# Loading late weights straight into freed weight buffers, and timing evictions, stores and divisions by modelled transfer landings, in a fused attention and MLP kernel

## The chip, the cores and the metric

The kernel runs on one core of one Trainium2 chip. The metric is the device time of one execution in microseconds (us). Kernels are compared by the median of their runs.

A core has five engines, each with an instruction queue that it works through strictly in order: TensorE (PE in the profile; its weight loads are PEld), VectorE (DVE), ScalarE (ACT), GpSimd (POOL) and SyncE (SP). In this kernel SP issues every DMA. An instruction that waits for a semaphore holds up all that stands behind it in the same queue.

## The reference

A gated mix of a sliding-window attention block and an MLP over the same 2048 tokens of width 512:

```python
def _A_ref(x, wqkv, wo):
    H = 32; Dh = D // H; W = 256
    qkv = (x @ wqkv).reshape(B, S, 3, H, Dh) ...
    scores = jnp.einsum("bhqd,bhkd->bhqk", q, k) * (Dh ** -0.5)
    mask = (idx[:, None] - idx[None, :] >= 0) & (idx[:, None] - idx[None, :] < W)
    p = _softmax(jnp.where(mask, scores, -1e9), axis=-1)
    o = jnp.einsum("bhqk,bhkd->bhqd", p, v)
    return o.transpose(...).reshape(B, S, D) @ wo

def _B_ref(x, w1, b1, w2, b2):
    h = _gelu(x @ w1 + b1)
    return h @ w2 + b2

g = _sigmoid((x * gate_w).sum(-1, keepdims=True))
return g * a + (1 - g) * b
```

Shapes: S = 2048, D = 512, F = 1792, all in float32.

## The kernel before

**Precision.** Every dense product is computed as three matmuls (`mm3`, lines 122 to 129): each operand is split into a high part, rounded to the PE's fp32r format, and a low part, the remainder, and the products high*high, high*low and low*high are added. So each weight is held as two tiles. ACT writes the high part (line 275) and DVE or POOL the low part by a subtraction (line 278), from a raw tile that a DMA has brought.

**Stages.** First q, k and v for four blocks of 512 tokens (`qkv`). Then two streams share the PE. The attention stream runs over 8 groups of 4 heads, each over the 16 blocks of 128 keys: `sm` tiles (scores for the row maximum, `att_max`, line 652; DVE reduces each into `M`, line 656), `st` tiles (transposed scores, `att_exp`, line 708; ACT takes the exponential into `pt`, line 737), and every fourth block a batch of `pv` products (`att_pvs`, line 764), which are copied out as `nd` (lines 784 and 787). The dense stream is the MLP in eight turns, `TURNS`: the first half of F for token blocks 3, 0, 1, 2 and the second half for 2, 0, 1, 3. A turn computes seven `u` tiles with w1, takes each through a gelu of seven steps on ACT and DVE (`gelu`; it ends with `h`, lines 921 and 924), and then four `y` tiles with w2. Each `y` is evicted by DVE (`y_end`, line 1012) as `yo` = 0.5 y + `ya`, and `yo` is stored to DRAM (YA for the first half, YB for the second); `ya` is the bias in the first half and the stored YA row block in the second. Last come the output projection and the mix (`final`).

**Divisions.** Every second head group `att_norm` divides 16 numerators: it loads the denominators (`den`), takes the reciprocal (line 807), stores it (RD), loads it back in a broadcast form (`rb`) beside the numerators (`num`), multiplies (line 819) and stores the result (OT).

**What sets the order.** Nothing is reordered by a compiler. A planner in the kernel's Python code keeps a clock, `now[0]`, and emits the instructions of all engines in the order in which its model would run them. `put(e, ns, fn, wait, due, req, key)` queues an operation for DVE, ACT or POOL: it may be emitted from `now + wait` on, once all keys of `req` are marked; among those that may start the earliest due time goes first. `after(ns, fn)` calls a function later. `scores()` yields the attention stream, `dense()` the MLP stream; the loop at the end chooses between them by `owed`, the dense work that is due, within the bounds SLACK (1400 ns that dense may run ahead) and OVER (2000 ns that it may be behind).

**What the planner takes for a landing.** `send` emits a DMA on SP and adds 500 ns (ISSUE) to a line of issue. What depends on a transfer is called a fixed time later: `landed(ns, ...)`. For a division that is 6000 ns (`den`), 4500 ns (RD) and 9500 ns (`num`, `rb`), each after the last issue (DIVS). A `yo` is stored 4600 ns and the next-but-one `ya` loaded 4000 ns (HOLD) after its eviction is emitted. An eviction does not ask whether the store that used its buffer, or the load of its `ya`, has landed; nor do the `sm` and `st` matmuls ask for the landing of `qd` and `ks`. The hardware semaphores do: an instruction that comes too early waits at the head of its queue.

**Eight lanes.** The DMAs of SP take eight semaphores in turn. Each issue waits until the DMA eight places before it has landed, and until its own data are there, and then the DMAs behind it may go.

**Buffers.** Split weights lie in one pool, `w`, of 14 buffers, each with both parts (two times 128x512 float32). The late weights (w1, w2 and `wo`, the list `later`) are loaded as the weights of the stage before are used for the last time, at least 4000 ns (PACE) apart: up to 152 us on the plan's clock (RAWS) to halves of attention's `pt` buffers, after that to two `raw` buffers, which `slots` counts; a third load waits until the low part of one is computed and a pause REST has gone by. The gelu has two `x1` and two `sq` buffers, and `yo` shares `sq`.

## Time and profile before

| | us |
|---|---|
| median of 3 runs | 715.34 |
| lowest, highest | 712.29, 717.89 |
| profiled execution | 719.64 |
| its span, first to last instruction | 717.7 |

The profile is that of one execution; times in it are microseconds from the span's start. PE is busy in nearly all of the span, so what can be won is the time in which PE sits idle or runs at a lower clock. The profile writes idle time in square brackets behind the instruction that ended it, with what released it. PEclk is the granted clock, 1.00 being full speed. The stretch from 0 to about 100 us is the q, k and v work, 100 to 650 us holds both streams, and the output projection is the end.

### The profile page before, as it was taken

The numbers are of one execution on the slowest core, as the hardware profiler recorded it, in microseconds if no ns is written. First come the engines' busy times: TensorE is split into PE (matmuls) and PEld (weight loads), VectorE is DVE, ScalarE is ACT, GpSimd is POOL, SyncE is SP. The second block draws the span as 40 slices with busy tenths as digits, with TensorE's granted clock in tenths as the row PEclk, the third lists the DMA queues.
The fourth block names the chain that finished last, engine by engine and source line by source line (L and its number), as shares of the span: only waits on it lengthen the run. The fifth ranks groups of instructions, "written<-read, shape, count | busy, mean of one in ns | idle before, by whom it ended". The sixth has DMA issues, their size and how long they took to land.

```text
span 717.7 us, 17515 instructions
## 1 busy us (share of the span) xinstructions
PE 698.1 (97%) x6129; PEld 603.4 (84%) x6129; DVE 516.7 (72%) x1560; ACT 419.9 (59%) x972; POOL 362.6 (51%) x853
## 2 busy tenths in 40 slices
PE   9999999999899999999999999989999999999998
PEld 7888888878788888888888887878888887888786
DVE  4732425798668977986898799749967985884662
ACT  4434532378447945864696588338745863794740
POOL 4200001568665765795587668636865785540000
PEclk9999999998999999999999999999999999999999
DMA  8979899895896899899986998995899789766562
GB/s 289 360 240 384 279 360 294 260 287 168 233 262 149 213 254 269 227 237 290 249 192 169 235 248 198 254 269 125 207 251 256 191 219 266 204 199 192 183 210 103
DMA packets 178103, 169.99 MB, mean 237 GB/s; under 512 B 56544, under 2 KB 122848, under 8 KB 178016
## 3 DMA queue, kind: packets, MB, share of 16 engines
q1 hardware_dynamic: 178016, 168.87, 84.4%
q8 instruction: 49, 0.80, 0.5%
q14 instruction: 38, 0.31, 0.2%
HBM read 111.68 MB, written 61.34 MB: 241 GB/s over the span
## 4 chain that ended last, share of the span: by engine, by line
PE 82%; DMA 7%; DVE 6%; issue 2%; ACT 2%; SPq 1%; POOL 0%; DVEq 0%; POOLq 0%; ACTq 0%
PE sm L652 8%; PE st L708 8%; PE pv_sm L764 6%; PE u L127 6%; PE y L129 6%; PE y L127 6%; PE y L128 6%; PE u L128 5%; PE u L129 5%; PE qk L127 4%; PE qk L129 4%; PE qk L128 4%; DVE sm L656 3%; PE pv_st L764 2%; PE a L127 2%
## 5 line engine op out<-in xcount | busy, mean ns | idle before, releaser
L656 DVE CUSTOM_DVE_ANT_1 sm<-sm,mask 128x320 f32<-128x320 f32 (+4 forms) x512 | 232.5, 484 | 57.5 <-PE sm L652 52.5
L724 POOL TENSOR_SCALAR_AFFINE_SELECT pt<-pt 64x256 f32<-64x256 f32 (+1 forms) x538 | 205.1, 401 | 131.0 <-ACT pt L737 119.9
L737 ACT ACTIVATE pt<-st 128x320 f32<-128x320 f32 (+4 forms) x512 | 200.7, 426 | 116.2 <-PE st L708 114.9
L652 PE MATMUL sm<-kd,qd 96*128 96x320 f32 (+4 forms) x512 | 147.7, 301 | 5.1 <-DVE M L656 3.3
L708 PE MATMUL st<-qs,ks 128*128 128x320 f32 (+4 forms) x512 | 146.8, 299 | 3.2 <-issue 2.0
L688 POOL CAST qs<-tt 4x256 fp32r<-4x256 f32 x256 | 127.6, 498 | 27.9 <-DVE tt L680 16.2
L652 PEld LDWEIGHTS sm<-kd,qd 96*128 96x128 f32 x512 | 97.0, 189 | 22.0 <-DVE M L656 6.8
L708 PEld LDWEIGHTS st<-qs,ks 128*128 128x128 f32 x512 | 97.8, 191 | 14.5 <-issue 2.7
L129 PE MATMUL y<-w,h 128*128 128x512 f32 x224 | 85.0, 379 | 1.8 <-DVE h L924 1.8
L127 PE MATMUL y<-w,h 128*128 128x512 f32 x224 | 84.8, 379 | 0.0
L128 PE MATMUL y<-w,h 128*128 128x512 f32 x224 | 84.8, 378 | 0.0
L764 PE MATMUL pv_sm<-pt,vbuf 64*32 64x320 f32 (+4 forms) x1408 | 76.4, 357 | 3.2 <-DVE M L656 3.1
L127 PE MATMUL u<-mx,w 128*128 128x512 f32 x196 | 77.4, 395 | 0.1
L764 PE MATMUL pv_st<-pt,vbuf 64*32 64x320 f32 (+4 forms) x1408 | 75.7, 357 | 0.0
L129 PE MATMUL u<-mx,w 128*128 128x512 f32 x196 | 74.3, 379 | 0.0
L128 PE MATMUL u<-mx,w 128*128 128x512 f32 x196 | 74.2, 379 | 0.0
L764 PEld LDWEIGHTS pv_sm<-pt,vbuf 64*32 64x32 f32 x1408 | 52.2, 109 | 23.7 <-DVE M L656 5.3
L656 DVE DVE_READ_ACCUMULATOR2_ANT M<- 128x1 f32 x512 | 71.5, 140 | 0.0
L434 DVE TENSOR_TENSOR qke<-qk,qke 128x512 fp32r<-128x512 f32 x32 | 22.1, 691 | 41.0 <-ACT qke L431 34.7
L431 ACT ACTIVATE qke<-qk 128x512 fp32r<-128x512 f32 x32 | 19.1, 597 | 52.0 <-PE qk L129 32.4
L129 PEld LDWEIGHTS y<-w,h 128*128 128x128 f32 x224 | 42.2, 188 | 8.2 <-DVE h L924 2.2
L764 PEld LDWEIGHTS pv_st<-pt,vbuf 64*32 64x32 f32 x1408 | 46.9, 109 | 0.0
(150 smaller groups left out, 1294.2 us busy)
## 6 DMA issues: line engine op xcount, KB each, us to landing
kd<-SK SPq DMA_DIRECT2D x32, 384.0 KB
qs<-SQ SPq DMA_DIRECT2D x64, 192.0 KB
mx<-XT SPq DMA_DIRECT2D x24, 512.0 KB
SQ<-qke SPq DMA_DIRECT2D x16, 512.0 KB
SK<-qke SPq DMA_DIRECT2D x16, 512.0 KB
ND<-nd SPq DMA_DIRECT2D x32, 256.0 KB
raw_w<-in_B_w_dram SPq DMA_DIRECT2D x28, 256.0 KB
qd<-SQ SPq DMA_DIRECT2D x32, 192.0 KB
```

Of the source, the lines that this page charges most:

```text
L127: nc.tensor.matmul(p, lh, rh, start=first, stop=False)
L128: nc.tensor.matmul(p, lh, rl, start=False, stop=False)
L129: nc.tensor.matmul(p, ll, rh, start=False, stop=last)
L431: nc.scalar.activation(halves(e[:, h]), p, AF.Copy)
L434: nc.vector.tensor_sub(halves(e[:, 1 - h]), p, halves(f32(e[:, h])))
L652: nc.tensor.matmul(v, qd[0:96, n, pr, 128 * j:128 * (j + 1)], two(kd[0:96, n, pr, k1 - w:k1]), start=True, stop=True)
L656: nc.vector.tensor_tensor_reduce(v, v, two(mask[:, 320 - w:320]), 1.0, -3e38, ALU.add, ALU.max, M[:, 2 * (b % RB) + hb, pr:pr + 1])
L688: nc.gpsimd.tensor_copy(dst, src.unsqueeze(1).broadcast_to([4, 2, RB, 32]))
L708: nc.tensor.matmul(pairs(p[:, :w]), ks[:, slot(g_, kb // NB), pr, at:at + 128], two(qs[:, pr, k0:k0 + w]), start=True, stop=True)
L724: nc.gpsimd.affine_select(out=v, in_=v, pattern=[[0, v.shape[1]], [1 - 2 * e, 64]], compare_op=ALU.is_ge, fill=0.0, base=-e, channel_multi ...
L737: nc.scalar.activation(halves(pt[:, hf, pr, :w]), sorted_(p[:, :w]), AF.Exp, scale=SCALE)
L764: nc.tensor.matmul(pv[r // 64][32 * i:32 * i + 32, q - c * T:e - c * T], vts[g_, b // NB][r:r + 64, v:v + 32], rhs(r), start=start, stop=s ...
```

## The change

The same matmuls, transfers and vector operations are issued; two low parts move from DVE to POOL (12 subtractions of w on POOL before, 14 now). What changes is where the weights lie, and when the planner emits what.

- **Weights.** The pool `w` is replaced by 14 places for high parts (`wh`) and 15 for low parts (`wl0` to `wl14`), held by name in `idle_low`. When a weight has been used for the last time, `drop` returns its low place. A late weight is loaded straight to such a place; its low part goes to a second one, and then the first is returned. A load needs two idle places, and loads may follow each other every 1200 ns (PACEL). After 140 us (RAWS) the engine for a low part is the one of DVE and POOL that is less behind; before, it is POOL. The two `raw` buffers go, and `x1` gets a third.
- **Landings.** The planner models eight lanes. A transfer starts when its lane is free and ends after a time by kind: 5000 ns (LOADS), 7000 ns for broadcast and scattered ones (SLOW), 4000, 4400 and 3100 ns for `nd`, `den` and RD; 1200 ns (MARGIN) are added before anything relies on it.
- **Waits in the plan.** An eviction is emitted once its `ya` has landed and the store that used its buffer has; `sm` and `st` are emitted once `qd` and `ks` have; the divisions go by the landings above. A `yo` is stored 200 ns after its eviction and the next `ya` loaded 600 ns after.
- **Bounds.** SLACK and OVER become 4000 ns.

```diff
-    line = [0.0]
+    line, lanes, sent = [0.0], [0.0] * 8, [0]
 
-    def send(to, by):
+    def send(to, by, ns=LOADS):
 
         nc.sync.dma_start(to, by)
-        line[0] = max(line[0], now[0]) + ISSUE
-
-    def landed(ns, fn, *args):
-
-        after(line[0] + ns - now[0], fn, *args)
+        k = sent[0] = (sent[0] + 1) % 8
+        at = max(line[0], now[0], lanes[k])
+        line[0], lanes[k] = at + ISSUE, at + ns
+
+    def landed(fn, *args):
+
+        after(lanes[sent[0]] + MARGIN - now[0], fn, *args)
+
+    def arrive(key):
+
+        mark(key, lanes[sent[0]] + MARGIN)
...
+    def low_tile(dtype, name):
+
+        s = idle_low.pop(0)
+        return sb.tile([128, T], dtype, tag=f"wl{s}", bufs=1, name=name), s
+
+    def high_tile(dtype, name):
+
+        return sb.tile([128, T], dtype, tag="wh", bufs=14, name=name)
+
+    def drop(key):
+
+        idle_low.append(wt[key][2])
...
         else:
-            spare.clear()
-            raw = sb.tile([128, T], F32, tag="raw", bufs=2, name=f"raw_{kind}{i}")
+            raw, slots[key] = low_tile(F32, f"raw_{kind}{i}")
...
-        paced[0] = max(now[0], paced[0] + PACE)
+        paced[0] = max(now[0], paced[0] + (PACE if now[0] < RAWS else PACEL))
...
     def load_now():
-        if now[0] >= RAWS:
-            if slots[0] - slots[1] == 2:
-                return after(500, load_now)
-            slots[0] += 1
+        if len(idle_low) < 2:
+            return after(300, load_now)
         key = asked.pop(0)
         load_raw(key)
-        if now[0] >= RAWS:
-            landed(LAND, split, key, nc.vector, True)
-        else:
-            after(LAND0 + 3000, split, key, nc.gpsimd)
+        landed(split, key, nc.gpsimd if now[0] < RAWS else None)
...
     def load_qd(g_, c):
         ready(c, g_, 0)
         put_pairs([f32(qd[48 * s:48 * s + 48, slot(g_, c)]) for s in range(2)], SQ[c], g_)
+        arrive(("qd", g_, c))
...
+            reqs = [("ya", n * NB + b)]
...
-                y = sb.tile([128, D], F32, tag="sq", bufs=2, name=f"yo{t}_{half}{b}")
+                y, k = sq_of(f"yo{t}_{half}{b}", ("yos", n, b))
+                reqs += k
...
-            after(HOLD, ya_load, n * NB + b + 2)
...
+            def then():
+                after(YALD, ya_load, n * NB + b + 2)
+                if n + 1 < len(TURNS):
+                    after(YST, store)
+                else:
+                    ybs[t * NB + b] = y
+                    mark(("y", half, t, b))
+            put("V", 604, ev, 130, 500, req=reqs, key=("ye", n, b), then=then)
...
-                        yield (rings["st"][0], *rows_of(u // NKB, u % NKB, i))
+                        yield (rings["st"][0], ("ks", u // NKB, u % NKB // NB), *rows_of(u // NKB, u % NKB, i))
...
-                        yield (rings["sm"][0],)
+                        yield (rings["sm"][0], ("qd", gm, bm // NB))
...
-RAWS = 152000.0
+RAWS = 140000.0
+LOWS = 15
...
-DIVS = ((6000, 4500, 9500), (5000, 2500, 7000))
-REST = 1000.0
...
-SLACK = 1400.0
-OVER = 2000.0
+SLACK = 4000.0
+OVER = 4000.0
```

In a division the calls read `landed(first)`, `landed(both)` and `landed(times)` now, with the kinds 4400 for `den`, 3100 for RD and SLOW for `num` and `rb` given to `send`.

**DVE at the last gelu of the turn that loads the second w2.** The rows are in DVE's own order, with the program's names: `h2_12` and `h2_13` are low parts of the gelu's results, `x1h` a step before, `w2_13` the low part of a late weight, `num3_1` a division's product, `sm` a reduction of scores and `M` its result. Before:

```order
L924 TENSOR_TENSOR h2_12_6316<-x1h2_12_6316_6320,h2_12_6316 128x512
L918 SCALAR_TENSOR_TENSOR x1h2_13_6383_6389<-sqh2_13_6383_6390,x1h2_13_6383_6389 128x512
L278 TENSOR_TENSOR w2_13_6454<-raw_w213_6322,w2_13_6454 128x512
L924 TENSOR_TENSOR h2_13_6383<-x1h2_13_6383_6389,h2_13_6383 128x512
L819 TENSOR_TENSOR num3_1_6416<-num3_1_6416,rb3_1_6418 128x512
L656 ISA sm5_4_3_6541,M5_4_6482<-sm5_4_3_6541,mask_72 128x320
```

The low part of the turn's last weight stands between the last two gelu results, four to ten rows ahead of the first eviction. The same place now:

```order
L684 ISA sm5_3_1_6500,M5_0_6275<-sm5_3_1_6500,mask_72 128x320
L684 ISA M5_0_6275 128x1
L684 ISA sm5_3_0_6506,M5_0_6275<-sm5_3_0_6506,mask_72 128x320
L684 ISA M5_0_6275 128x1
L961 TENSOR_TENSOR h2_13_6410<-x1h2_13_6410_6417,h2_13_6410 128x512
L684 ISA sm5_3_3_6527,M5_0_6275<-sm5_3_3_6527,mask_72 128x320
```

No late weight stands there any more: DVE's last one in this turn, `w2l12`, stands 78 rows ahead of `h2_13` (916 against 994 from the queue's start), and `w2l13` went to POOL. `h2_12` stands 32 rows ahead of the first eviction `yo2_10`, where it stood 10 ahead.

**SP at the first stores of YB.** `yo2_10` and `yo2_11` are the first two evicted tiles of that turn. Before:

```order
L140 DMA ks_74<-SK3_1_94 48x8x128
L140 DMA ks_74<-SK3_1_94 48x7x128
L140 DMA ks_74<-SK3_1_94 48x2x64
L140 DMA vbuf_158<-SV2_97 128x8x34
L140 DMA ND1_2_113<-nd4_1_6598 128x512
L140 DMA mx40_6384<-XT0_99 128x1024
L140 DMA ya2_12_6681<-YA2_141 128x512
L140 DMA YB2_145<-yo2_10_6627 128x512
```

And now:

```order
L140 DMA mx40_6411<-XT0_99 128x1024
L140 DMA YB2_145<-yo2_10_6562 128x512
L140 DMA ya2_12_6599<-YA2_141 128x512
L140 DMA ks_74<-SK3_1_94 48x8x128
L140 DMA ks_74<-SK3_1_94 48x7x128
L140 DMA ks_74<-SK3_1_94 48x2x64
L140 DMA vbuf_158<-SV2_97 128x8x34
L140 DMA ND1_2_113<-nd4_1_6654 128x512
```

The store of `yo2_10` and the load of `ya2_12` stand ahead of the `ks`, `vbuf` and `ND` transfers, behind which they stood. On DVE the eviction that takes `yo2_10`'s buffer, `yo2_12`, stands 37 rows behind `yo2_10`, where it stood 29 rows behind.

**PE ahead of the first `st` that needs the third block of `ks`.** `st0_8_0` is that matmul; `y3_00` and `y3_01` are dense tiles. Before:

```order
L127 MATMUL y3_01_2155<-w2_3_1845,h3_3_1789 128x512
L128 MATMUL y3_01_2155<-w2_3_1845,h3_3_1789 128x512
L129 MATMUL y3_01_2155<-w2_3_1845,h3_3_1789 128x512
L652 MATMUL sm1_4_1_2216<-kd_76,qd_75 128x320
L708 MATMUL st0_8_0_2219<-qs_73,ks_74 128x320
```

And now:

```order
L127 MATMUL y3_01_2206<-w2h3_1853,h3_3_1777 128x512
L128 MATMUL y3_01_2206<-w2l3_2000,h3_3_1777 128x512
L129 MATMUL y3_01_2206<-w2h3_1853,h3_3_1777 128x512
L680 MATMUL sm1_4_1_2250<-kd_76,qd_75 128x320
L127 MATMUL y3_01_2206<-w2h4_1864,h3_4_1856 128x512
L128 MATMUL y3_01_2206<-w2l4_1933,h3_4_1856 128x512
L129 MATMUL y3_01_2206<-w2h4_1864,h3_4_1856 128x512
L736 MATMUL st0_8_0_2259<-qs_73,ks_74 128x320
```

One dense product, three matmuls, has come ahead of `st0_8_0`. Between the last `sm` of head group 0 (`sm0_15_2`, which reads the `kd` buffer that SP writes next) and `st0_8_0` stand 36 `y` matmuls where there were 33; the other work between the two is the same.

## Prediction

> **What bounds the kernel now.** I read the totals first, then the waits of PE and of DVE, then the timeline around each PE wait.

> ```profile
> span 717.7 us, 17515 instructions
> PE 698.1 (97%) x6129; PEld 603.4 (84%) x6129; DVE 516.7 (72%) x1560; ACT 419.9 (59%) x972; POOL 362.6 (51%) x853
> ```

> PE is the bound: only 717.7 - 698.1 = 19.6 us of the span are free of matmuls. No work is taken away, so the change can win only PE's idle time and what follows from it. Who ends that idle time (us in total, times, longest):

> ```profile
> PE sm L652 <- DVE M L656: 3.3, 4, 1.3
> PE pv_sm L764 <- DVE M L656: 3.1, 2, 2.7
> PE st L708 <- issue: 2.0, 1, 2.0
> PE y L129 <- DVE h L924: 1.8, 1, 1.8
> ```

> PE waits for DVE most times: a score tile's PSUM buffer comes free when DVE has reduced it. DVE's own waits for transfers are therefore the next view:

> ```profile
> DVE yo L1012 <- DMA YB<-yo: 5.2, 2, 3.3
> DVE num L819 <- issue: 3.0, 2, 2.0
> DVE yo L1012 <- PE sm L652: 2.7, 1, 2.7
> DVE yo L1012 <- DMA YA<-yo: 2.1, 1, 2.1
> DVE yo L1012 <- DMA ya<-YA: 1.7, 1, 1.7
> DVE num L819 <- DMA rb<-RD: 1.2, 1, 1.2
> ```

> Evictions (`yo`) stand 5.2 + 2.7 + 2.1 + 1.7 = 11.7 us at the head of DVE's queue, the divisions' multiplications (`num`) 4.2. The largest case in the timelines of SP, DVE and PE (start, length, engine, what; idle before in brackets):

> ```profile
> 464.75 0.42 SPq L140 DMA_DIRECT2D YB<-yo  x1
> 469.50 0.69 DVE L1012 SCALAR_TENSOR_TENSOR yo<-y,ya 128x512 f32<-128x512 f32 x1 [3.25 <-DMA YB<-yo]
> 470.71 0.30 PE L764 MATMUL pv_sm<-pt,vbuf 64*32 64x64 f32 x2 [2.74 <-DVE M L656]
> ```

> The store of the first `yo` is issued at 464.75 and lands some 4.7 us later; the third eviction needs its buffer and waits 3.25 us; the reductions behind it come late, and PE stands 2.74 us. Then the clock falls (columns: stretch, its length, busy time of PE, PEld, DVE, ACT, POOL, granted clock, DMA):

> ```profile
> 160.70:167.50 6.80, 5.93 (x15) 4.84 (x16) 4.01 (x7) 4.17 (x9) 5.65 (x8) 0.50 0.67 146
> 191.40:194.80 3.40, 3.40 (x67) 1.77 (x73) 0.56 (x2) 0.44 (x1) 0.95 (x3) 0.50 1.06 280
> 471.30:474.70 3.40, 3.40 (x75) 2.50 (x58) 0.26 (x2) 0.00 (x0) 0.00 (x0) 0.50 1.11 298
> ```

> The granted clock is 0.50 in three stretches, 13.6 us together, each behind a PE wait. Half of that, up to 6.8 us, is lost on top of the idle time.

> **The change part by part.** The sum is made against this execution, 719.64 us (its span and 1.9 around it). It lies 4.3 above the median, 715.34.

> *Evictions and stores.* The PE waits behind a `yo` that waits:

> ```profile
> 206.86 0.40 PE L652 MATMUL sm<-kd,qd 96*128 96x320 f32 x1 [0.50 <-DVE M L656]
> 329.97 1.55 SPq L140 DMA_DIRECT2D YA<-yo  x1
> 334.58 0.69 DVE L1012 SCALAR_TENSOR_TENSOR yo<-y,ya 128x512 f32<-128x512 f32 x1 [2.66 <-PE sm L652]
> 335.79 0.40 PE L652 MATMUL sm<-kd,qd 96*128 96x320 f32 x1 [1.08 <-DVE M L656]
> 337.66 0.30 PE L764 MATMUL pv_sm<-pt,vbuf 64*32 64x64 f32 x2 [0.40 <-DVE M L656]
> 664.87 0.73 PE L708 MATMUL st<-qs,ks 128*128 128x320 f32 x2 [0.98 <-ACT nd L784]
> ```

> The eviction at 334.58 is put down to an `sm`, but it starts 4.6 us after a YA store was issued, as the one above came 4.75 after its store; I count it here. The change issues the store 200 ns after an eviction instead of 4600 after its emission, ahead of the `ks` loads (SP's order), and emits the next user of the buffer 37 instead of 29 DVE rows later. PE's part: 0.50 + 1.08 + 0.40 + 2.74 + 0.98 = 5.70, with half of the last slow stretch, 1.70, 7.4 us. Bounds: 3.7, if half returns behind other landings, and 7.4. I take 7.4, because both distances grow in the order. What is late next is the reduction itself.

> *Landing of `ks`.* The SP and PE rows:

> ```profile
> 160.57 11.46 SPq L140 DMA_DIRECT2D kd<-SK  x2
> 183.01 0.32 SPq L140 DMA_DIRECT2D mx<-XT  x1
> 183.38 1.72 SPq L140 DMA_DIRECT2D ks<-SK  x3
> 190.22 0.38 PE L708 MATMUL st<-qs,ks 128*128 128x320 f32 x1 [2.00 <-issue]
> 168.38 0.38 PE L127 MATMUL u<-xt,w 128*128 128x512 f32 x1
> 168.59 0.38 PE L128 MATMUL u<-xt,w 128*128 128x512 f32 x1
> ```

> SP holds `kd` until PE has read the old tile, then `mx` until the XT stores have landed, and `ks` stands behind both. The plan models neither stop. By PE's order only three matmuls of 0.21 us (start to start, 168.38 to 168.59) come in between: 0.65 of the 2.00 goes. Bounds: 0, and 2.00 + 1.70 with its slow stretch. I take 0.65, what the order shows.

> *Late weights.* At the last gelus of the turn that loads the second w2:

> ```profile
> 443.73 0.81 DVE w L278
> 446.52 0.40 PE L652 MATMUL sm<-kd,qd 96*128 96x320 f32 x1 [0.47 <-DVE M L656]
> 449.26 0.48 PE L129 MATMUL y<-w,h 128*128 128x512 f32 x1 [1.76 <-DVE h L924]
> ```

> The first row is of the chain of work that ended last: a weight's low part, 0.81 us, in DVE's queue ahead of the `h` for which PE stands. In the new order no weight is split there, and `h2_12` stands 32 rows ahead of the first eviction, not 10. PE's waits are 2.23 us; I take 2.0, bounds 0 and 2.23. The split costs the same, on ACT and, two more times, on POOL. The loads now come in a burst: five raw loads among nine consecutive issues. Behind them stand `qs`, a division's loads and `kd`. No row shows that; the nearest is the `ks` stop, 2.0 us, or 3.7 with its slow stretch; below, nothing. I charge 2.0.

> *The first gelus beside attention.*

> ```profile
> 159.22 0.40 PE L652 MATMUL sm<-kd,qd 96*128 96x320 f32 x1 [0.60 <-DMA qd<-SQ]
> 161.57 0.80 PE L127 MATMUL u<-xt,w 128*128 128x512 f32 x1 [1.20 <-DVE sqh L912]
> ```

> With half of 6.80 that is 5.2 us. The plan now asks for `qd`, and lets dense run further ahead, but DVE's work there is the same. Bounds 0 and 5.2; I take the middle, 2.6, since one of the two causes is met. The wider SLACK and OVER I cost at nothing else: they move matmuls between two streams, and either covers the other.

> *Divisions.* They are now called sooner: 8.2 us after `rb` is issued instead of 10.0, 5.6 instead of 6.5 after `den`, where lanes are free. PE's share in them before, and one more wait of an eviction:

> ```profile
> 556.50 0.40 PE L652 MATMUL sm<-kd,qd 96*128 96x320 f32 x1 [0.93 <-DVE nd L787]
> 603.93 0.40 PE L652 MATMUL sm<-kd,qd 96*128 96x320 f32 x1 [1.30 <-DVE M L656]
> 314.22 0.60 SPq L140 DMA_DIRECT2D rb<-RD  x1
> 322.30 0.77 DVE L819 TENSOR_TENSOR num<-num,rb 128x512 f32<-128x512 f32 x1 [1.22 <-DMA rb<-RD]
> ```

> This `rb` took 8.1 us, about what the plan now allows. I charge 1.0, bounds +0.93 won and 17.5 lost (the slower rival). Of the 1.30 I take half, 0.6, bounds 0 and 1.3, for DVE there waited for PE's own `y`.

> Sum: 7.4 + 0.65 + 2.0 - 2.0 + 2.6 - 1.0 + 0.6 = 10.25, which gives 709.4 for an execution like this one. The median before lies 4.3 lower, by waits of the same kind that partly did not happen; I take half of it off: 707.2.

> [...] The slow stretches of 3.40 us follow PE waits of 2.00 and 2.74. [...]

> **Rivals.**

> *DVE takes the place of the transfers.* For it speaks this window:

> ```profile
> 350.00:400.00 50.00, 50.00 (x503) 43.95 (x502) 46.64 (x149) 38.40 (x88) 39.54 (x90) 1.00 0.83 198
> ```

> DVE is busy 93% of it, and what it does not lose to landings it has to do anyway. Against it: PE lost nothing in that stretch. If half of the evictions, weights and gelus (12.0) returns, 6.0, the time is 713.2.

> *The clock does not follow the waits.* If slow stretches come at another cause's bidding, 1.7 of the evictions and 1.7 of the gelus stay: 710.6. Against it: three of three stand behind a wait.

> *The change doesn't do what it says, and DVE waits for divisions instead.* With 1.8 us less at 12 multiplications and 0.9 less at 16 reciprocals, DVE would stand up to 36 us more; PE lost 5.70 for 11.7 at the evictions, so 0.49 of that, 17.5, less the 1.0 charged: 723.7, slower. It decides from the point at which most `rb` land later than 8.2 us after their planned issue. For it: the 8.1 above. Against it: at 13 of 16 multiplications DVE did not wait at all, and a plan with lanes waits longer when they are full.

> **How the numbers follow.** My forecast has 0.48, the DVE rival 0.30, the clock 0.08, the divisions 0.14. The measurement can tell about 1% from no change: faster is below 708.2, slower above 722.5. So 0.48 faster, 0.38 the same, 0.14 slower. The range: all gains at their best, no charges: 7.4 + 3.7 + 2.23 + 5.2 + 1.3 + 0.93 = 20.8, 698.9, rounded to 700; evictions at 3.7, the others 0, the burst at 3.7 and divisions at 1.0: 720.6, on the median 718.5. I take 700 to 718; the slower rival is left out.

> **What would show it.** Right: no DVE wait of an eviction for YA or YB; no wait of a `y` matmul for `h`; fewer stretches at 0.50. `st` for the third `ks` still waits a microsecond or more. Wrong: new waits of `num` or `den` for `rb` or `den`, PE waits behind the raw loads, or PE idle time near 19.6 us again.

## The result, and the profile after

The changed kernel takes 703.39 us (median of 6 runs, 701.76 to 705.12), the kernel before 715.31 in the same runs: ratio 0.9839, 95% interval 0.9805 to 0.9872. It is faster by 1.6%, inside the predicted range and 3.8 us under the predicted 707.2. The profiled execution took 704.36 us, 15.28 less than that of before; that execution of before was a slow one, 4.3 us above its median, so 3.4 of the 15.28 go beyond the 11.9 between the medians. The totals of its page:

```profile
span 702.4 us, 17477 instructions
PE 691.5 (98%) x6129; PEld 594.1 (85%) x6129; DVE 514.4 (73%) x1558; ACT 416.5 (59%) x972; POOL 364.9 (52%) x855
```

The span without matmuls is 702.4 - 691.5 = 10.9 us, where it was 19.6: 8.7 less. PE's busy time is 6.6 less for the same 6129 matmuls: no stretch at half clock is left before the end, where there were 13.6 us. Together 15.3. Who ends the waits now, in the views of PE's and of DVE's waits (us in total, times, longest):

```profile
PE st L736 <- DMA ks<-SK: 1.7, 1, 1.7
...
PE st L736 <- ACT nd L812: 0.8, 1, 0.8
PE sm L680 <- DVE M L684: 0.8, 2, 0.5
...
PE y L129 <- DVE h L961: 0.5, 1, 0.5
```

```profile
DVE yo L1056 <- DMA ya<-YA: 3.7, 2, 2.1
...
DVE yo L1056 <- DMA YA<-yo: 1.8, 1, 1.8
```

The waits of `pv_sm` for `M` are gone, those of `sm` fell from 3.3 to 0.8 us, that of `y` for `h` from 1.8 to 0.5. Evictions still stand 5.5 us for transfers (11.7 before, with the 2.7 that was put down to an `sm`), but PE pays nothing for it that the rows show. No PE wait stands right behind the first two of the three cases. One stands behind the third; DVE's, ACT's and PE's rows there:

```profile
647.45 0.69 DVE L1056 SCALAR_TENSOR_TENSOR yo<-y,ya 128x512 f32<-128x512 f32 x1 [2.06 <-DMA ya<-YA]
...
647.99 1.91 ACT L922 ACTIVATE ot<-ot 128x512 fp32r<-128x512 f32 x3 [3.06 <-DMA ot<-OT]
649.81 0.58 ACT L812 ACTIVATE nd<-pv_st 128x512 f32<-128x512 f32 x1
...
650.44 0.40 PE L736 MATMUL st<-qs,ks 128*128 128x320 f32 x1 [0.80 <-ACT nd L812]
```

PE waits for `nd`, which stands in ACT's queue behind three `ot`, and ACT waited 3.06 us for their load. So this wait comes from the loads of the output projection and not from the eviction.

The largest wait that is left is the one for the third block of `ks`. SP and PE:

```profile
179.94 0.32 SPq L140 DMA_DIRECT2D mx<-XT  x1
180.31 2.46 SPq L140 DMA_DIRECT2D ks<-SK  x3
...
186.69 0.37 PE L736 MATMUL st<-qs,ks 128*128 128x320 f32 x1 [1.73 <-DMA ks<-SK]
```

`ks` goes as soon as `mx` has gone, as before, and its first transfer is issued 6.4 us ahead of PE's start. This wait is not there in every profile of such a kernel: see e9.

### The profile page after: what moved, and what is told of

It is laid out like the page before. It is cut to its first block, busy times and chain, and to the rows that moved or that the text cites. A ratio compares the mean times of both kernels' runs of the same rounds, so it can differ in the third digit from the quotient of the medians.

```text
span 702.4 us, 17477 instructions
## 1 busy us (share of the span) xinstructions
PE 691.5 (98%) x6129; PEld 594.1 (85%) x6129; DVE 514.4 (73%) x1558; ACT 416.5 (59%) x972; POOL 364.9 (52%) x855
## 4 chain that ended last, share of the span: by engine, by line
PE 85%; DMA 7%; DVE 2%; ACT 2%; issue 1%; POOL 1%; SPq 1%; POOLq 0%; DVEq 0%; ACTq 0%
PE sm L680 9%; PE st L736 8%; PE pv_sm L792 7%; PE y L127 6%; PE y L129 6%; PE y L128 6%; PE u L127 6%; PE u L128 5%; PE u L129 5%; PE qk L127 4%; PE qk L129 4%; PE qk L128 4%; PE a L127 2%; PE a L129 2%; PE a L128 2%; PE v L127 2%
## 5 line engine op out<-in xcount | busy, mean ns | idle before, releaser
L752 POOL TENSOR_SCALAR_AFFINE_SELECT pt<-pt 64x256 f32<-64x256 f32 (+1 forms) x538 | 208.9, 408 | 110.6 <-ACT pt L765 99.7
L765 ACT ACTIVATE pt<-st 128x320 f32<-128x320 f32 (+4 forms) x512 | 191.9, 427 | 108.3 <-PE st L736 105.0
L736 PE MATMUL st<-qs,ks 128*128 128x320 f32 (+4 forms) x512 | 143.1, 297 | 2.9 <-DMA ks<-SK 1.7
L716 POOL CAST qs<-tt 4x256 fp32r<-4x256 f32 x256 | 123.9, 484 | 27.5 <-DVE tt L708 15.9
L129 PE MATMUL y<-w2h,h 128*128 128x512 f32 x224 | 85.1, 380 | 0.8 <-DVE h L961 0.5
L127 PE MATMUL y<-w2h,h 128*128 128x512 f32 x224 | 85.1, 380 | 0.0
L128 PE MATMUL y<-w2l,h 128*128 128x512 f32 x224 | 84.8, 378 | 0.0
L127 PE MATMUL u<-mx,w1h 128*128 128x512 f32 x196 | 76.9, 393 | 0.2 <-DVE sqh L949 0.2
L129 PE MATMUL u<-mx,w1l 128*128 128x512 f32 x196 | 74.3, 379 | 0.0
L128 PE MATMUL u<-mx,w1h 128*128 128x512 f32 x196 | 74.2, 379 | 0.0
L792 PE MATMUL pv_sm<-pt,vbuf 64*32 64x320 f32 (+4 forms) x1408 | 73.3, 346 | 0.1
L453 ACT ACTIVATE qke<-qk 128x512 fp32r<-128x512 f32 x32 | 19.1, 598 | 51.5 <-PE qk L129 28.6
L129 PEld LDWEIGHTS y<-w2h,h 128*128 128x128 f32 x224 | 42.2, 188 | 7.3 <-DVE h L961 1.3
```

The lines of the kernel that those rows point to most:

```text
L127: nc.tensor.matmul(p, lh, rh, start=first, stop=False)
L128: nc.tensor.matmul(p, lh, rl, start=False, stop=False)
L129: nc.tensor.matmul(p, ll, rh, start=False, stop=last)
L453: nc.scalar.activation(halves(e[:, h]), p, AF.Copy)
L716: nc.gpsimd.tensor_copy(dst, src.unsqueeze(1).broadcast_to([4, 2, RB, 32]))
L736: nc.tensor.matmul(pairs(p[:, :w]), ks[:, slot(g_, kb // NB), pr, at:at + 128], two(qs[:, pr, k0:k0 + w]), start=True, stop=True)
```

## The experiments

Each kernel was timed beside the kernel before on the same chip, in three groups: c1 and e1 to e3; e4 to e7; e8 to e11. Three of them (c1, e4, e9) came out level with the changed kernel, so they mark it on their chips: 703.91, 702.61 and 702.86 us; costs below are against these. The changed kernel itself was not timed again beside them; by its ratio to the kernel before, 0.984, the costs of e1 to e3 would come out 1.5 us higher, that of e8 0.8 higher and those of e5 to e7 0.5 lower. "Plan" is the planner's own clock (`now[0]`) at the end of its loop, in us: what the kernel's code takes the PE stream to need, no measured time. "Clock" is what half clock took from a run on average, at most, since PE may also idle in such a stretch: (1 - mean granted clock) x span, from the clocks listed with every run.

| kernel | median us | runs | before | ratio (95%) | plan | clock |
|---|---|---|---|---|---|---|
| before, beside c1 to e3 | 713.95 | 29 | | | 686.7 | 4.1 |
| changed | 703.39 | 6 | 715.31 | 0.984 (0.981 to 0.987) | 686.7 | 0.4 |
| c1 margin 50 ns more | 703.91 | 6 | 713.95 | 0.986 (0.982 to 0.990) | 686.6 | 0.5 |
| e1 evictions undone | 708.68 | 12 | 713.95 | 0.995 (0.992 to 0.998) | 685.9 | 1.1 |
| e2 late stores, asking | 709.64 | 12 | 713.95 | 0.994 (0.992 to 0.997) | 689.5 | 1.2 |
| e3 narrow bounds | 711.31 | 12 | 713.95 | 0.996 (0.993 to 0.999) | 692.9 | 1.1 |
| e4 early stores, not asking | 702.61 | 6 | 714.57 | 0.982 (0.979 to 0.985) | 686.7 | 0.0 |
| e5 qd, ks not asked for | 706.65 | 6 | 714.57 | 0.989 (0.985 to 0.992) | 688.4 | 3.9 |
| e6 slow weights | 712.68 | 12 | 714.57 | 0.996 (0.994 to 0.998) | 694.8 | 4.2 |
| e7 late divisions, longer lanes | 720.55 | 6 | 714.57 | 1.008 (1.005 to 1.011) | 709.1 | 6.4 |
| e8 late divisions | 707.88 | 12 | 713.55 | 0.993 (0.990 to 0.995) | 692.0 | 1.4 |
| e9 ks first | 702.86 | 5 | 713.55 | 0.987 (0.985 to 0.990) | 686.7 | 0.3 |
| e10 before, wide bounds | 718.62 | 9 | 713.55 | 1.007 (1.004 to 1.010) | 685.8 | 5.3 |
| e11 before, early stores | 711.29 | 12 | 713.55 | 0.997 (0.995 to 1.000) | 686.5 | 3.4 |

**c1, a control.**

```diff
-MARGIN = 1200.0
+MARGIN = 1250.0
```

> The changed kernel with MARGIN 1250 ns instead of 1200: every landing that the plan waits for is taken 50 ns later, which reshuffles thousands of rows and means nothing by itself. Every theory expects the changed kernel's time, 703.4 us, within 1.5, and no granted clock under 1.00 after the start. If it is further off than that, differences of the same size between the other kernels may come from the reshuffling alone.

As expected: 703.91, though one of the six runs has a mean clock of 0.997. This reshuffling moved the time by 0.5 us, and e4 and e9 stay within 1, so I take a difference of 4 us and more for that of an edit. Three reshuffled kernels make that likely; they are no bound.

**e1 and e2, evictions as before, and the late times alone.**

```diff
-            reqs = [("ya", n * NB + b)]
+            reqs = []
...
-YALD = 600.0
-YST = 200.0
+YALD = 3256.0
+YST = 3856.0
```

In e1 the gelu's question for its `sq` buffer is left out as well. The late times are those of the store and of the next `ya` load, together.

> The changed kernel with the evictions as before: they ask for no landing, the store goes 4.6 us after the eviction, the load of the next ya 4.0 us after; gelu asks for no store either. Theory evictions (the prediction's largest term: 5.70 us of PE idle time and 1.70 of slow clock): 710.8 us (708 to 712), DVE standing 5 us or more in all at yo for YA or YB, PE idle 14 us or more. Theory bounds (the wider SLACK and OVER let PE do the other stream while DVE stands): 703.4 to 705, DVE standing all the same, PE idle near 11 us.

> The changed kernel with the late times alone put back (store 4.6 us after the eviction starts, ya 4.0 us after), while evictions still ask for the landings in the plan. Theory evictions in the form that the early store wins: 707 to 711, since the buffer comes free 3.7 us later and DVE or the plan has to wait that long. In the form that asking wins: 703.4 to 705.5, with DVE standing under 3 us at yo for transfers.

e1 lost 4.8 us against c1 and 5.3 against 703.4, within the 708 to 712 of the theory of evictions. DVE's and PE's waits in e1:

```profile
DVE yo L1055 <- DMA YB<-yo: 9.3, 3, 5.9
...
DVE yo L1055 <- DMA YA<-yo: 7.2, 2, 4.2
...
DVE yo L1055 <- DMA ya<-YA: 4.4, 1, 4.4
```

```profile
PE sm L680 <- DVE M L684: 5.8, 3, 2.8
```

DVE stands 20.9 us for transfers. Of PE's 5.8 us, 5.4 follow two of these evictions (at 200.83 and 589.74 us); the third case, 0.47, is there in the changed kernel too. The wide bounds do not cover that. e2 keeps the questions and costs the same, 5.7. Here DVE stands only 3.7 for transfers (3.5 for YA, 0.2 for YB), but the plan is 2.8 us longer: what the chip waits for in e1, the plan waits for in e2. So it is the early times that win, as the form with 707 to 711 says. Store and `ya` load were not moved one without the other; that the store counts most is read from e1's rows, where 16.5 of the 20.9 us, and both of PE's long waits, stand behind a store.

**e4, early stores without asking.** The edit of `reqs` alone, and the gelu's question for `sq` left out.

> The changed kernel with early stores kept, but evictions that ask for no landing (nor gelu for the store of its buffer). Since putting the late times back cost as much as undoing both (709.64 and 708.68 us), theory early store: this costs nothing, 702.5 to 704.9, and DVE stands at yo for transfers no longer than now, 5.5 us. Theory asking: 706 or more.

702.61: the evictions' asking buys nothing once the store goes early. With c1's spread that is no gain over the changed kernel either.

**e3, the bounds as before.**

```diff
-SLACK = 4000.0
-OVER = 4000.0
+SLACK = 1400.0
+OVER = 2000.0
```

> The changed kernel with SLACK 1400 and OVER 2000 ns as before. The prediction gave the bounds nothing beyond half of the first gelus' 5.2 us: 703.4 to 706. Theory bounds: 708 to 712, with PE idle time back to 15 us or more, u waits for sqh above 1 us near the first gelus and stretches of the clock at 0.50.

711.31, 7.4 above c1: inside the 708 to 712 of the theory of bounds, and outside what the prediction gave. PE's rows, the two longest waits:

```profile
182.93 0.48 PE L129 MATMUL y<-w2h,h 128*128 128x512 f32 x1 [1.78 <-DVE h L961]
...
195.92 0.48 PE L127 MATMUL y<-w2h,h 128*128 128x512 f32 x1 [1.74 <-issue]
```

PE's idle time is 15.7 us (10.9 in the changed kernel), as that theory has it, and half clock costs 1.1 us on average. PE is also busy 2.9 us longer (694.4 against 691.5), at full clock in this profile; no row explains that part. The other marks that it named, waits of `u` for `sqh` near the first gelus and a slow stretch in the profile, did not come. What came is in the table: the plan itself is 6.2 us longer. By the code, with narrow bounds a stream whose operand the plan knows to be missing holds PE, since the other stream may not run further ahead.

**e10, wide bounds on the kernel before.** The same two lines, the other way, in the kernel before.

> The kernel before with SLACK and OVER 4000 alone. Theory bounds alone: undoing them cost 7.9 us, so 706 to 708 against the 714.3 of before. Theory that they pay only where the plan sees that an operand is missing (its evictions, qd and ks are not asked for here): 712 to 715, PE idle time near 19 us.

718.62: 5.1 us slower than before, outside both expectations. The plan is 0.9 shorter, the chip is not. The runs spread from 713.35 to 720.52 and the profiled one, with a span of 712.1, is at their lower end, so its rows do not show what the median lost. PE's longest waits:

```profile
190.08 0.44 PE L708 MATMUL st<-qs,ks 128*128 128x320 f32 x1 [3.06 <-DMA ks<-SK]
...
335.70 0.40 PE L652 MATMUL sm<-kd,qd 96*128 96x320 f32 x1 [2.04 <-DVE M L656]
...
552.69 0.40 PE L652 MATMUL sm<-kd,qd 96*128 96x320 f32 x1 [2.23 <-DVE nd L787]
```

These are three waits of before (2.00, 1.08 and 0.93 us), each about 1 us longer, the places unchanged. Two others are gone: that of `u` for `sqh` near 161 us falls from 1.20 to 0.21, and that of `y` for `h` near 449 us, 1.76 before, is not there, although DVE splits the same weight ahead of the same `h`. So the bounds are worth 7.4 us in the changed kernel and lose 5.1 in the kernel before. That the asking makes this difference fits e3's plan and the expectation's second theory in kind; it is not shown, since the two kernels differ in the other parts too.

**e5, qd and ks not asked for.**

```diff
-                        yield (rings["st"][0], ("ks", u // NKB, u % NKB // NB), *rows_of(...))
+                        yield (rings["st"][0], *rows_of(...))
...
-                        yield (rings["sm"][0], ("qd", gm, bm // NB))
+                        yield (rings["sm"][0],)
```

> The changed kernel with sm and st not asking for the landing of qd and ks in the plan. The prediction gave the question for ks 0.65 us and that for qd half of 5.2: so 704.0 to 706.7, with PE waits of st for ks of 2.0 us or more in all and of sm for qd near 160 us. Theory bounds (the wider bounds help because the plan now sees that an operand is missing and sends the other stream): as much as undoing the bounds, 708 to 712.

706.65, 4.0 above e4: near the upper end of the prediction's terms (706.7), below that of the bounds. Where it goes the profiles do not settle: every run of e5 has a slow stretch (at most 3.9 us a run on average, none in e4), but PE's idle time is 704.5 - 692.1 = 12.4 us, 3.2 more than in e4 and 1.5 more than in the changed kernel, and its busy time is no longer than in e4 (692.3). The windows around the wait (length, busy PE, PEld, DVE, ACT, POOL, granted clock, DMA share, GB/s):

```profile
177.98:181.39 3.41, 2.01 (x9) 1.09 (x8) 3.41 (x13) 2.59 (x6) 3.25 (x7) 1.00 0.99 273
181.39:184.80 3.41, 1.80 (x6) 1.64 (x6) 3.02 (x13) 0.89 (x3) 3.08 (x10) 0.50 1.20 242
184.80:188.21 3.41, 3.41 (x9) 2.69 (x8) 0.31 (x1) 0.00 (x0) 2.54 (x6) 0.50 1.03 265
```

Several short waits and the one for `ks` (1.61 us) fall together here, and 6.8 us run at half clock. PE is busy in only 5.2 of them, so they cost some 2.6 us beside the waits. No wait for `qd` appeared.

**e6, slow weights.**

```diff
-PACEL = 1200.0
+PACEL = 4000.0
...
-        if len(idle_low) < 2:
-            return after(300, load_now)
+        if len(idle_low) < 2 or now[0] >= RAWS and len(slots) > 1:
+            return after(500, load_now)
...
-        landed(split, key, nc.gpsimd if now[0] < RAWS else None)
+        landed(split, key, nc.gpsimd if now[0] < RAWS else nc.vector)
```

> The changed kernel with late weights slow, about as before: loads at least 4.0 us apart, at most two raw tiles after 140 us, low parts on DVE. The prediction had 2.0 us won and 2.0 charged for the burst: 703.4 within 1.5. Theory weights (no burst cost, so the gain stands alone): 705 to 707, with waits of y for h or the weight's low part of 1 us and more in the turns that load weights.

712.68, 10.1 above e4, more than any theory said. PE's rows:

```profile
182.70 0.79 PE L128 MATMUL y<-w2l,h 128*128 128x512 f32 x1 [3.08 <-DVE w2l L305]
...
446.33 0.55 PE L129 MATMUL y<-w2h,h 128*128 128x512 f32 x1 [1.51 <-DVE h L961]
```

The second is the wait of before at 449 us, back at its place. The first isn't one of before: the edit limits the loads from 140 us on, where the kernel before went on into the `pt` halves up to 152, so SP issues the last late weight of the first turn at 185.82 here; before, its last row of such loads started at 159.41. The run overstates the part. What it shows of the second turn is 1.51 us and the slow stretch behind it, 1.7. Even there slow weights alone are not the cause: e10 has them too, with wide bounds, and not this wait.

**e7 and e8, divisions called later.** e7 tells the plan longer kinds (nd 4300, den 5300, RD 3800, num and rb 8800), e8 adds the time only to the calls:

```diff
-    def landed(fn, *args):
+    def landed(fn, *args, more=0):
...
-        after(lanes[sent[0]] + MARGIN - now[0], fn, *args)
+        after(lanes[sent[0]] + MARGIN + more - now[0], fn, *args)
...
-            landed(both)
+            landed(both, more=700)
...
-            landed(times)
+            landed(times, more=1800)
...
-        landed(first)
+        landed(first, more=900)
```

> The changed kernel with a division's steps called as late as before: den 5300, RD 3800, num and rb 8800 ns, nd 4300. The prediction charged 1.0 us for the sooner calls: 702.4. Theory that they cost nothing: 703.4 within 1.5. Theory that sooner divisions win: 705 or more, the end of the kernel waiting for the last ot.

> The changed kernel with a division's steps called 0.9, 0.7 and 1.8 us later, the times of the kernel before, but with the lanes modelled as in the changed kernel (the earlier run with late divisions, at 720.55 us, also told the plan that these transfers hold their lanes longer). Theory lanes (the plan's lanes, inflated, moved everything else): 703.4 within 1.5 here. Theory calls (the sooner calls themselves win, the opposite of the 1.0 us that the prediction charged): 710 or more, with PE waits near 333, 383, 430 and 440 us as in the earlier run.

e7 took 720.55, 17.9 above e4. I had not foreseen that: a kind that is too long fills the plan's lanes, so everything behind it is planned later (plan 709.1). e8 took 707.88, 5.0 above e9, between its two theories. PE's rows of e7, then of e8:

```profile
333.20 0.37 PE L680 MATMUL sm<-kd,qd 96*128 96x320 f32 x1 [2.44 <-DMA qd<-SQ]
...
383.68 0.25 PE L792 MATMUL pv_st<-pt,vbuf 64*32 64x64 f32 x2 [1.93 <-POOL pt L752]
...
429.77 0.53 PE L680 MATMUL sm<-kd,qd 96*128 96x320 f32 x1 [2.04 <-DVE M L684]
...
440.56 0.79 PE L127 MATMUL u<-mx,w1h 128*128 128x512 f32 x1 [2.65 <-DVE sqh L949]
```

```profile
312.04 0.48 PE L129 MATMUL y<-w2h,h 128*128 128x512 f32 x1 [1.23 <-DVE h L961]
...
427.38 0.77 PE L127 MATMUL u<-mx,w1h 128*128 128x512 f32 x1 [2.25 <-DVE sqh L949]
```

Of e7's four waits at most one, between 427 and 441, comes back in e8, and 12.9 of the 17.9 us with it do not: most of e7 was the lanes. e8 also delays the four divisions with c = 3 beyond the times of before, which were shorter for them (DIVS, second row), and part of its cost is at the end of the plan (5.3 longer). So no cost of the sooner calls shows, and what they win is not settled.

**e9, ks ahead of mx.**

```diff
-            load_x(TURNS[n + 1][1], f"mx{n}")
+            after(8000 if n == 0 else 0, load_x, TURNS[n + 1][1], f"mx{n}")
```

> The changed kernel with the first loads of mx called 8 us later in the first turn, so that the three ks loads go to SP ahead of them and no longer behind the XT stores' landing. The prediction left 1.35 us of the ks wait because SP stops at mx: if so, PE's 1.7 us wait of st for ks goes (0.3 or less) and the time is 701.7 (701 to 703). Rival: the wait goes but the next turn's u waits for its later mx, 703.4 or more. Rival: ks lands no sooner, the wait stays at 1.7.

SP, then ACT and PE near the end of the dense work:

```profile
168.44 3.45 SPq L140 DMA_DIRECT2D XT<-xt  x4
171.99 2.96 SPq L140 DMA_DIRECT2D ks<-SK  x3
...
646.06 1.95 ACT L922 ACTIVATE ot<-ot 128x512 fp32r<-128x512 f32 x3 [4.22 <-DMA ot<-OT]
...
648.55 0.40 PE L736 MATMUL st<-qs,ks 128*128 128x320 f32 x1 [1.99 <-ACT nd L812]
```

`ks` goes 8.3 us sooner, since it no longer stands behind `mx`. The wait of 1.73 is gone, but that alone doesn't show the stop at `mx` to be its cause, for it is gone in c1, e1, e2, e4 and e8 too, where `mx` still goes first. There SP comes to `ks` at 177.27 to 179.00 us, in the changed kernel's profile at 180.31. c1's row:

```profile
178.16 1.71 SPq L140 DMA_DIRECT2D ks<-SK  x3
```

So with the stop at `mx`, 1.3 us sooner or later seem to decide whether PE waits. The median, 702.86, is inside the 701 to 703 of the first reading, but the ratios of the two kernels overlap, so no gain is shown. In this profile another wait has grown: ACT waits 4.22 us for the loads of `ot` instead of 3.06, and PE stands 1.99 at 648.55 instead of 0.80 at 650.44.

**e11, early stores on the kernel before.**

```diff
-            after(HOLD, ya_load, n * NB + b + 2)
+            after(1344, ya_load, n * NB + b + 2)
...
-                after(HOLD + 600, store)
+                after(944, store)
```

> The kernel before with the store issued 200 ns after an eviction's end and the next ya load 600 ns after, nothing else. The prediction's largest term: 7.4 us of the profiled execution, so 707 to 709 against 714.3, with DVE standing under 4 us at yo for YA and YB. Theory that the early store pays only beside the other parts: 712 or more.

711.29, a gain of 2.3 us (0.3%, interval 0.04% to 0.5%), where 5 to 7 were expected; the rival's 712 is nearer, though the time lies between the two. The waits of `yo` for YA and YB are gone from DVE's list. Others stand there (first fence), and in PE's rows of the timeline (second):

```profile
DVE den L807 <- DMA den<-ND: 5.9, 3, 4.3
...
DVE den L807 <- DMA qd<-SQ: 2.7, 1, 2.7
```

```profile
415.16 0.40 PE L652 MATMUL sm<-kd,qd 96*128 96x320 f32 x1 [1.35 <-DVE nd L787]
...
443.06 0.80 PE L129 MATMUL y<-w,h 128*128 128x512 f32 x1 [1.77 <-DVE h L924]
...
532.80 0.40 PE L652 MATMUL sm<-kd,qd 96*128 96x320 f32 x1 [2.24 <-DVE M L656]
...
550.62 0.40 PE L652 MATMUL sm<-kd,qd 96*128 96x320 f32 x1 [1.74 <-DVE nd L787]
```

The reciprocals wait 8.6 us in these two rows and 9.7 in all, where they waited 3.4 in all before. Three of the four PE waits shown (at 415.16, 532.80 and 550.62) follow a reciprocal that waited 0.87, 4.26 and 2.66 us. That the earlier stores moved the divisions' transfers, whose calls are at fixed times, is my reading; no run tests it. The wait for `h` stays, 1.77, with weights and bounds as before.

## Why the prediction was right, and where not

The direction, the range and the likeliest case were right. The sum was 10.25 us against the profiled execution, which got 15.28. The three terms that held back most, 2.0 for the burst, 1.0 for the divisions and the half of the first gelus that I left standing, 2.6, make 5.6; none of the three losses occurred. That the sum came out as near as it did is in part luck: its largest term was too high, and one that it put at nothing, the bounds, costs 7.4 us when it is undone.

- **Evictions and stores, 7.4.** The mechanism was right: the early times are what wins (e1, e2, e4). In the profile all these waits are gone but one of 0.80 for `nd`, which now has another cause. As a price the size was high: undoing it costs 4.8, alone it gains 2.3. "No DVE wait of an eviction for YA or YB" was nearly right: one of 1.8 us for YA remains.
- **Landing of ks, 0.65.** Near the profile, partly by luck. 1.73 of the 2.00 us are left there, where 1.35 would have been, and SP does stop at `mx`, as the term says. But in c1, e1, e2, e4 and e8 the whole wait is gone, with `ks` behind `mx` as before.
- **Late weights, 2.0 won and 2.0 charged.** The wait went: none of `y` for `h` is left near 449 us (one of 0.5 stands at 176), and e6 and e11 show it at its place where weights are slow or left as they were. That the low part in DVE's queue was its one cause isn't shown: it takes 0.81 us of the 1.76, and with the wide bounds alone (e10) the wait went without any change of the weights. The charge was wrong: no wait behind the raw loads appeared. Undoing cost 10.1, an overstatement for the reason given, so the net of nothing was too low, by an amount that isn't settled.
- **The first gelus, 2.6.** Too low. `u` waits 0.4 us there at the longest and nothing is at half clock, so 4.8 of the 5.2 went. e5 gives 4.0 for asking, though at another place: 20 us later, where waits fall together and the clock follows. The wait of `u` itself is down to 0.2 with the bounds alone (e10) and with everything but the bounds (e3), so there they are enough and not needed.
- **The bounds, nothing.** This step failed: the bounds cost 7.4 us when undone in the changed kernel and lose 5.1 when set alone in the kernel before, so they were far from nothing both ways. I read it so that "either covers the other" holds only while the plan knows which stream is ready; e3's plan, 6.2 us longer, fits that, and e10's loss is not explained by its rows.
- **Divisions, 1.0 charged.** No such loss came: `num` has no wait left (4.2 us before), and later calls make the kernel slower, not faster (e8). Whether the sooner calls win anything stays open, for the reason given at e8.
- **The rivals.** DVE didn't take the place of the transfers. The clock followed the waits: its share is up to 4.1 - 0.4 = 3.7 us of the 11.9 between the medians. The waits for divisions of the third rival did not come in the changed kernel; in e11, where the early stores stood alone, such waits (9.7 us of reciprocals) did, with divisions called as before.

The working failed in one thing that no term shows: it added up parts as if each could be priced alone. Undone one at a time they cost 4.8 (e1), 7.4 (e3), 4.0 (e5), 10.1 (e6) and 5.0 (e8), 31 us, and all together gained 12; e6 and e8 undo more than their part, but the other three alone make 16. The column of the plan points to why. The plan is as long as before (686.7 us), so nothing was won in it; what shrank is the chip's distance from it, from 28.6 us (715.3 - 686.7) to 16.7. Kernels whose stores are late and not asked for stand 22.8 (e1), 28.6 (before) and 32.8 us (e10) above their plan, and e11, with early stores but no asking, 24.8. The changed kernel's other variants stand 15.9 to 20.1 above (c1, e2 to e6, e8, e9); e2 asks with late stores, e4 has early stores without the evictions' questions, and e5 leaves out those for `qd` and `ks`. e7, whose plan allows the transfers more time, stands 11.5 above. Where a part is missing but the plan knows of it (e3, e6, e8), the plan gets longer, by 5 to 8 us, and the chip follows. My reading is that each part covers a wait that another would bring back. That the plan waits is read from its code and length; it was not tried with only the asking and the bounds on the kernel before.

## What to carry to other kernels

In a hand-planned kernel, compare the plan's own length with the measured time before pricing single waits: here an honest plan won from that distance, and where wide bounds or early stores were missing (e3, e2) the wait moved from the chip into the plan. A bound that pays in one such kernel can cost in another (e3, e10), so try such parts together and alone. Storing a shared buffer, and loading the next one, right behind the operation that fills it won in both kernels, 5.7 us (e2) and 2.3 (e11). And before a wait is put down to a part, look at the profile of a kernel that should be level: the wait for `ks` is in the changed kernel's and not in c1's, 50 ns of margin apart.

## What the runs showed of the hardware

```profile
585.30:588.71 3.41, 1.65 (x37) 0.98 (x20) 0.18 (x1) 0.93 (x2) 1.59 (x5) 1.00 1.04 292
588.71:592.12 3.41, 2.38 (x14) 2.22 (x15) 3.04 (x11) 0.87 (x2) 0.00 (x0) 1.00 1.15 253
592.12:595.53 3.41, 3.41 (x21) 3.09 (x20) 1.92 (x8) 1.42 (x4) 1.56 (x4) 1.00 1.29 181
```

```profile
423.64:427.05 3.41, 1.49 (x8) 0.98 (x6) 3.34 (x8) 1.23 (x3) 3.13 (x8) 1.00 0.47 136
427.05:430.46 3.41, 3.08 (x10) 2.75 (x11) 2.43 (x10) 2.41 (x6) 2.75 (x6) 0.50 0.65 215
```

```profile
382.10:385.51 3.41, 1.53 (x57) 1.20 (x65) 1.37 (x5) 0.00 (x0) 3.09 (x10) 1.00 0.81 174
385.51:388.92 3.41, 3.41 (x51) 2.58 (x36) 0.00 (x0) 0.60 (x1) 2.25 (x6) 0.50 0.00 0
```

The longest of the three waits is split by a border of the grid, 1.76 and 1.03 us idle, and the clock stays at 1.00; 1.92 and 1.88 us inside one step are followed by 0.50 in the next. I laid the grid on the traces of all 14 kernels from 20 to 690 us, from the edges of their clock, and took PE's idle time in each step at full clock: all 10 steps with more than 1.8 us were followed by 0.50, 4 of the 32 with 0.9 to 1.8, and none of some 2690 with less. Two of the traces in single steps: in before, 0.50 came behind 2.74, 2.00 and 0.99 us of idle time and not behind 1.76, 1.43 and 1.30; in the changed kernel the most was 1.39, at the wait for `ks`, and no 0.50 came. Between 0.9 and 1.8 us the idle time alone doesn't decide here: steps with 0.99 (before), 1.40 (e5) and 1.51 us (e6) were followed by 0.50, one with 1.79 (e3) was not. The grid's first edge lies 7.08 us behind the span's start in before and 4.40 in the changed kernel, from 3.9 to 7.3 in the 14 profiles, so the same wait falls differently, and so does the time lost.
